# Two attention chunks run as halves of 64 tokens, with a new order of all operations

## The chip, the core and the metric

The kernel runs on one core of one Trainium2 chip. The metric is the time of one execution on the device, in microseconds (us). A core has engines with instruction streams of their own, each worked off in order: TensorE (PE; its weight loads are PEld), VectorE (DVE), ScalarE (ACT), GpSimd (POOL), and SyncE (SP), which here issues the transfers (DMA).

## The reference

Three layers, one after the other, on q, k, v of 2 batches, 8 heads, 768 tokens and 64 columns in float32:

```
# 1. attention with decay, blocks of 64 tokens, per head
intra = (q_b @ k_b.T * Dmask) @ v_b ;  inter = (q_b * lam_pow) @ kv_state
out   = intra + inter
kv_state = lam**64 * kv_state + (k_b * rev_pow).T @ v_b
# 2. channel mix: x_prev is x shifted by one token, d_ff = 1024
xk, xr = mu_k*x + (1-mu_k)*x_prev, mu_r*x + (1-mu_r)*x_prev
x = sigmoid(xr @ w_r) * (relu(xk @ w_k)**2 @ w_v)
# 3. gated convolution with 5 taps
y = (sigmoid(conv(x)) * (x @ w_val)) @ w_out
```

The weights of layers 2 and 3 arrive as 64-bit floats.

## The kernel before

**Chunks.** Attention runs over 12 chunks of 128 tokens, 0 to 5 for the first batch and 6 to 11 for the second, each for all 8 heads. A chunk has operations named by a letter and its number: Tk and Tq (PE transposes of k and q, chunks 0 to 5 only), Ek and Eq (ACT copies of these out of PSUM), Q (q times powers of lam), D (k times decays), S (scores), M (DVE: scores times the mask), U (the update of the state), O and N (state times decay, plus the update), Z (the result; for halves Y and Z), X (the result copied to SBUF). The function `whole` treats the chunk as one block of 128 tokens; `halves` treats it as two blocks of 64. `BIG` says which chunks are whole:

```
676         x, keep_x = (whole if c < BIG else halves)(c, b, cc)
494                     e.matmul(su[:, s, C * n:C * n + C], kt[half[s], n, :], qt[half[s], n, :], ...)
571                         e.matmul(su[half[j], s, Q * n:Q * n + Q], kt[half[s], n, t], qt[half[s], n, t], ...)
```

In `whole`, S is 8 products of 128 by 128 tokens (L494), U 8 (L516), Z 16 (L553), M one DVE multiplication of 128x1024 (L501), and the state is multiplied and added once (O at L531, N at L534). In `halves`, S is 16 products of 64 by 64 tokens (L571), U 16 (L592), Y 8 and Z 24 (L655), M 128x512 (L578), and there are two pairs of O and N, named O2.0, N2.0, O2.1, N2.1 (L613, L616). Z of halves begins with a drain of PE (L662). Each float32 product is two instructions in the trace. Both write their scores to the PSUM tile su and their result to xx. The update of `halves` lies in su too, that of `whole` in a buffer of its own.

**Weights.** A piece of 128x512 64-bit numbers is loaded (w0 to w19; y and z for layer 3) and turned into a high and a low float32r part by steps a to f, h and l: a, b and h on ACT, c, d and e on DVE, f and l on DVE or POOL. w0 to w3 belong to w_r, w4 to w11 to w_k, w12 to w19 to w_v.

**Products.** The channel mix goes over three groups of 512 tokens (pr 0, 1, 2). mr and mk are the mixed inputs (steps a, b, h, l); r, k and v the products, where `k0.2.1` is group 0, block 2, second half of the sum. A unit is 6 matmuls of 128x512 (12 of 128x256 for r of group 0), a third each for high by high, high by low, low by high. g are the gates (DVE), a and p the products of layer 3. Their accumulators turn in 4 PSUM buffers.

**Order.** ORDER is a list, written out in the source, of all 1070 operations; each engine gets its own in that sequence, with the engine after the colon where there is a choice (V, A, G for DVE, ACT, POOL). A load waits in SP's stream until its SBUF buffer is free. An operation on POOL waits for the last DVE operation that stands before it in the list (L249 to L254).

Of the kernel before, what the change touches and what calls it, by code (L numbers as in the profile page):

```python
# [18 lines left out]


ORDER = """
    zero table eye lam scan warm7 w3 w3b w3a w3c w3d w3e w1 w2 w1a w2a q0 Tq0 w1b warm3 w3f:V
# [11 lines left out]
    mr0.2.1h mr0.2.1l:V w9 w6d mk0.2a:A mk0.2b v5 mk0.0h w7c w7b Z4 w6b mk0.0l:V k6 r0.10.0
    r0.10.1 r0.10s mk0.1h mk0.2h w7d mk0.3b r0.11.0 w5l:V w6e mk0.1l:V w7e r0.11.1 mk0.3h
    mk0.3l:V w9a w7f:V r0.11s w9c w6f:V r0.00s w8 w7h mk0.2l:V w8a w8c w11 w6h w7l:V w11a
    w6l:V D6:V w10a w10c O5.0:V U5 v6 w9d w8d k0.2.0 w10b w13 k0.0.0 w9e X4:A w11c w13b w11b
# [2 lines left out]
    k0.1.1 w9l:V w12a w11f:V k0.2e:A k0.0q:A jq3.0 jk3.2 w12c w10f:V w11h w12d w11l:G jk3.3  # L40
    X5:A Bq3 w10h jk3.1 w10l:V w13d k0.0l:V jk3.0 k0.1e:A k0.1h w12e k0.6.0 N6.0:A k0.2h
    O6.1:V H2:A k7 w12f:V w13e k0.1q:A k0.2q:A k0.4.0 Q6:G Bk3 k0.5.0 k0.5.1 k0.5e:A k0.7.0
    k0.5h w13f:V k0.7.1 k0.1l:V S6 k0.7e:A w12h D7:G H3 k0.7h N6.1 w15 M6 w15a w14 w13h w15b
    v7 k0.5q:A w14a w12l:V k0.3h k0.3q:A Q7:V w15c Y6 k0.4.1 w13l:V w15d k0.6.1 Z6 O7.0:V w14c
    S7 w15e w14b w14d w15f:V w14e U7 k0.3l:V w17 k0.4e:A X6:A w14f:G w16 k0.6e:A M7 w15h w18
    v0.3.0 w19 N7.0 w17a v0.0.0 w15l:V k0.6h w17c w16a w16c w14h w17d v0.1.0 Y7 w16d k0.4h
    k0.4q:A Z7 v0.2.0 X7:A w18a w14l:V jk4.0 v9 k0.2l:V w16e w17e k0.4l:V w16b w19b w16f:V x0
    w18c k0.5l:V v0.2.1 k0.7q:A w17b w17f:V w16h v0.3.1 w19a w19c w16l:V w17h jq4.3 w18b
    w17l:V H4:A w18d v0.1.1 w19d mk1.1a:A w18e w19e w18f:V mk1.3a:A v0.0.1 w19f:V k0.6q:A
    mk1.0a:A k0.6l:V v0.2.2 k0.7l:V jk4.2 w18h w19h w19l:V w18l:V jk4.1 jq4.1 v0.0.2 v0.1.2  # L50
    mk1.0b v0.3.2 mk1.2a:A mk1.3b v0.1.3 mr1.1a:A v0.0.3 v0.2.3 mk1.0h mk1.1b k8 mk1.0l:V
# [6 lines left out]
    k1.4.1 k1.5.1 mr1.1l:G k1.2e:V mr1.2a:A O10.0:V k1.2h N10.0 O10.1:G N10.1 Q10:V M10 k1.6.1
    X9:V k11 D11:V k1.1q:V z3 mr1.2b mr1.2h mr1.2l:G r1.3.0 k1.0q:V x1.3:A v11 Y10 S11 k1.4e:A
    k1.4h Z10 X10:A U11 x1.2:A k1.7h mr1.3h O11.0:V N11.0 M11 k1.6e:A k1.1l:V mr1.3l:G k1.6h  # L60
    r1.1.0 k1.2q:V z0 k1.5e:A Y11 Z11 X11:V H5:G r1.2.0 mk2.0a:V x3 mk2.0b r1.2.1 mk2.0h
    r1.3.1 k1.0l:V mk2.1a:V mk2.1b k1.3h k1.3q:A k1.4q:G r1.2s r1.1.1 r1.1s v1.3.0 r1.3s y0
    r1.0.0 r1.0.1 mk2.3a:A v1.0.0 k1.2l:G k1.3l:V v1.3.1 k1.4l:G mk2.2a:V k1.5h y0a mk2.2b
    k1.5q:V z3a k1.5l:V v1.2.0 r1.0s k1.7q:A v1.0.1 k1.6q:V k1.6l:G k1.7l:V v1.1.0 v1.1.1
    v1.1.2 z0a z0c mr2.1a:A z0d mk2.1h mk2.0l:G mr2.0a:V mr2.3a:V y3 y3a y3c mr2.1b y3d mk2.2h
    y0c v1.2.1 mk2.1l:G mk2.3b v1.1.3 v1.1e v1.0.2 v1.0.3 v1.0e mr2.1h mr2.1l:V mk2.3h mr2.3b
    mk2.3l:V y2 y2b v1.2.2 v1.3.2 v1.2.3 y2a k2.1.0 mk2.2l:G y2c cw cwb cwa k2.4.0 cwc v1.2e
    cwd x4.2:V v1.3.3 k2.4.1 cwe cwf:V mr2.0b z3c x1.1:A z3d y1b v1.3e k2.2.0 z3e k2.4e:A y0d
    cwg cwt y1a y1c y1d y1e y3b z3b k2.1.1 g1.2.0:A z3f:V y0e mr2.2a:V k2.6.0 y2d y2e k2.1e:V
    g0.2.0:A mr2.0h k2.3.0 k2.3.1 k2.6.1 x2.3:V y1f:V z0e k2.5.0 g1.3.0:A g1.3.1 g0.3.0:A y0b  # L70
    k2.3e:A y0f:G g1.3.2 k2.5.1 y2f:G k2.5e:V k2.7.0 mr2.3h k2.6e:A k2.0.0 mr2.2b k2.3h k2.0.1
    x1.0:V k2.3q:A mr2.0l:G mr2.2h mr2.2l:V k2.2.1 k2.0e:A k2.3l:V k2.4h x2.1:A y3e y3f:V
    r2.3.0 k2.2e:A g0.2.1 mr2.3l:V g0.3.1 k2.7.1 k2.2h k2.0h g0.1.0:A g0.3.2 g0.3.3 x2.0:V
    g0.1.1 g0.1.2 k2.0q:A k2.2q:A k2.2l:V r2.1.0 k2.1h z0b k2.0l:V r2.2.0 r2.2.1 r2.1.1 r2.2s
    r2.0.0 r2.0.1 g1.0.0:V k2.1q:V k2.1l:V r2.3.1 k2.7e:A k2.7h g1.0.1 k2.5h k2.5q:V k2.5l:V
    g1.0.2 r2.0s k2.7q:A k2.4q:A z0f:V r2.3s s0.0h k2.6h v2.0.0 y1h v2.2.0 g1.2.1 g1.2.2
    v2.1.0 k2.4l:V v2.1.1 g1.3.3 g1.3.4 y2h r2.1s v2.3.0 y1l:V g0.2.2 v2.0.1 k2.7l:V v2.3.1
    g0.1.3 g0.0.0:A v2.3.2 v2.1.2 y2l:V v2.0.2 v2.2.1 v2.2.2 z1 k2.6q:V k2.6l:V v2.3.3
    g1.1.0:A y3h g1.1.1 z1a z1c g1.3s g0.0.1 y0h s0.2h s1.1h y0l:V g0.0.2 y3l:V s1.3h s1.1l:V
    z2 g1.0.3 s1.0h s0.0l:G g1.0.4 g0.0.3 g0.1.4 g0.1s s1.0l:G v2.1.3 s1.2h v2.1e v2.3e s0.1h  # L80
    z3h v2.0.3 s1.3l:V s0.3h s0.1l:V s1.2l:V g0.0.4 v2.2.3 g0.0s s0.2l:V a1.3.0 z0h g1.2.3
    a1.0.0 v2.0e a1.3.1 s0.3l:G a1.3e z1d z1e g1.0s a1.0.1 a1.0e z2a z3l:G a0.0.0 g0.2.3 z2c
    g0.2.4 a0.2.0 g0.2s z2d a0.1.0 a0.1.1 a0.1e z2e a0.2.1 z0l:V g1.2.4 z1b z1f:V z2b a0.3.0
    a0.0.1 a0.2e a0.3.1 a0.0e a0.2h a0.0h g0.3.4 a0.2l:V g0.3s z2f:G x5.1:A a1.2.0 a1.1.0
    v2.2e a0.1h a1.1.1 a0.3e a0.1l:V a0.3h x5.0:A a1.2.1 z2h a0.3l:V a0.0l:V z1h z1l:V z2l:V
    p0.0.0 x4.0:A p0.0.1 g1.1.2 g1.1.3 x5.2:A g1.1.4 g1.2s a1.3h p0.0e:V a1.3l:G g1.1s
    g2.2.0:A x4.3:A a1.1e a1.0h s2.2h g2.0.0:V p0.1.0 p0.1.1 p1.1.0 p1.0.0 g2.0.1 p0.1e:A
    g2.0.2 a1.1h a1.1l:V p1.0.1 p1.1.1 a1.0l:V x4.1:A g2.1.0:A a1.2e a1.2h g2.1.1 p2.1.0
    x5.3:V g2.3.0:A p0.0o p1.1e:A a1.2l:V s2.1h p1.0e:A g2.0.3 g2.3.1 g2.3.2 p2.1.1 g2.3.3
    g2.3.4 g2.3s p2.1e:A s2.1l:V p0.1o p3.1.0 s2.0h p3.1.1 g2.0.4 g2.0s p3.0.0 p3.0.1 p1.1o  # L90
    p3.1e:A p3.1o g2.1.2 s2.0l:V a2.1.0 g2.1.3 p2.0.0 p2.0.1 g2.1.4 a2.0.0 p3.0e:A g2.2.1
    g2.2.2 g2.2.3 a2.2.0 s2.3h s2.2l:G s2.3l:V a2.1.1 g2.2.4 p3.0o a2.0.1 g2.2s g2.1s a2.1e
    a2.0e a2.2.1 a2.1h a2.2e a2.3.0 a2.1l:V a2.3.1 a2.0h a2.0l:V a2.3e p4.0.0 a2.2h a2.2l:V
# [1000 lines left out]
```

## Time and profile before

| | |
|---|---|
| median of 3 runs | 290.45 us (290.04 to 290.76) |
| profiled execution | 290.39 us, of which 288.6 us from the first to the last instruction (the span) |
| PE busy | 275.2 us (95%) |
| DVE, ACT, POOL busy | 235.4 us (82%), 164.1 us (57%), 49.3 us (17%) |
| granted TensorE clock | 1.000 in every slice |
| chain that ended last | 90% PE, 5% DMA, 3% DVE |

The profile is one execution. A time in it counts from the span's first instruction; 1.8 us of the execution's own time lie around the span. The chain is followed back from the last instruction, at each step to what released it or to the instruction before it on its engine.

### The profile page before, as it was taken

The numbers are of one execution on the slowest core, as the hardware profiler recorded it, in microseconds if no ns is written. First come the engines' busy times: TensorE is split into PE (matmuls) and PEld (weight loads), VectorE is DVE, ScalarE is ACT, GpSimd is POOL, SyncE is SP. The second block draws the span as 40 slices with busy tenths as digits, with TensorE's granted clock in tenths as the row PEclk, the third lists the DMA queues.
The fourth block names the chain that finished last, engine by engine and source line by source line (L and its number), as shares of the span: only waits on it lengthen the run. The fifth ranks groups of instructions, "written<-read, shape, count | busy, mean of one in ns | idle before, by whom it ended". The sixth has DMA issues, their size and how long they took to land.

```text
span 288.6 us, 5971 instructions
## 1 busy us (share of the span) xinstructions
PE 275.2 (95%) x2345; PEld 229.1 (79%) x2345; DVE 235.4 (82%) x402; ACT 164.1 (57%) x309; POOL 49.3 (17%) x59
## 2 busy tenths in 40 slices
...
DMA packets 63626, 29.25 MB, mean 101 GB/s; under 512 B 58322, under 2 KB 58606, under 8 KB 63598
## 3 DMA queue, kind: packets, MB, share of 16 engines
...
q14 instruction: 10, 0.08, 0.1%
HBM read 25.72 MB, written 3.15 MB: 100 GB/s over the span
## 4 chain that ended last, share of the span: by engine, by line
PE 90%; DMA 5%; DVE 3%; ACT 1%; issue 1%; SPq 0%; DVEq 0%; ACTq 0%
PE b_k L754 23%; PE b_v L754 23%; PE b_r L754 12%; PE b_p L942 11%; PE b_a L754 11%; PE xx L655 4%; DMA b_v<-in_v_dram 2%; DMA xx<-in_moe_w_r_dram 2%; PE su L592 2%; PE su L571 1%; PE su L494 1%; PE xx L553 1%; PE b_Tq L440 1%; DVE xx L342 0%; DVE b_k L480 0%
## 5 line engine op out<-in xcount | busy, mean ns | idle before, releaser
L894 DVE SCALAR_TENSOR_TENSOR b_g<-xx,cw,b_g 128x512 f32<-128x512 f32 x48 | 38.5, 810 | 0.6
L754 PE MATMUL b_k<-b_mk_2h,w_rk 128*128 128x512 f32 x48 | 19.0, 397 | 0.0
L754 PE MATMUL b_r<-b_mr_0h,w_rk 128*128 128x256 f32 (+1 forms) x80 | 19.0, 312 | 0.0
L754 PE MATMUL b_k<-b_mk_0h,w_rk 128*128 128x512 f32 x48 | 18.9, 394 | 0.0
L754 PE MATMUL b_k<-b_mk_3h,w_rk 128*128 128x512 f32 x48 | 18.7, 390 | 0.0
L754 PE MATMUL b_k<-b_mk_1h,w_rk 128*128 128x512 f32 x48 | 18.7, 390 | 0.0
L902 ACT ACTIVATE b_g<-b_g 128x512 f32<-128x512 f32 x12 | 7.4, 628 | 16.6 <-DVE b_g L894 16.5
L754 PEld LDWEIGHTS b_r<-b_mr_0h,w_rk 128*128 128x128 f32 x80 | 13.2, 191 | 0.9
L869 DVE TENSOR_TENSOR xx<-b_v,xx 128x512 f32<-128x512 f32 x12 | 8.0, 687 | 6.4 <-PE b_v L754 6.4
L754 PE MATMUL b_r<-b_mr_0l,w_rk 128*128 128x256 f32 (+1 forms) x40 | 12.2, 305 | 0.0
L616 DVE TENSOR_TENSOR state<-su,state 128x256 f32<-128x256 f32 x13 | 5.5, 424 | 6.4 <-PE su L571 3.6
L754 PEld LDWEIGHTS b_k<-b_mk_2h,w_rk 128*128 128x128 f32 x48 | 9.0, 188 | 2.0
L754 PEld LDWEIGHTS b_k<-b_mk_0h,w_rk 128*128 128x128 f32 x48 | 9.0, 188 | 1.9
L754 PEld LDWEIGHTS b_k<-b_mk_3h,w_rk 128*128 128x128 f32 x48 | 9.0, 188 | 1.9
L754 PEld LDWEIGHTS b_k<-b_mk_1h,w_rk 128*128 128x128 f32 x48 | 9.0, 188 | 1.9
L440 PE MATMUL b_Tq<-ident,b_q 128*128 128x128 f32 x24 | 4.3, 309 | 5.6 <-DMA b_q<-in_q_dram 5.6
L754 PE MATMUL b_v<-b_k_0h,w_v 128*128 128x512 f32 x24 | 9.6, 399 | 0.0
L330 ACT ACTIVATE xx<-xx 128x512 int32<-128x512 uint32 x12 | 7.9, 668 | 2.9 <-DMA xx<-in_moe_w_r_dram 2.9
L754 PE MATMUL b_v<-b_k_1h,w_v 128*128 128x512 f32 x24 | 9.4, 391 | 0.0
L754 PE MATMUL b_k<-b_mk_2l,w_rk 128*128 128x512 f32 x24 | 9.4, 390 | 0.0
L754 PE MATMUL b_k<-b_mk_3l,w_rk 128*128 128x512 f32 x24 | 9.4, 390 | 0.0
L754 PE MATMUL b_k<-b_mk_0l,w_rk 128*128 128x512 f32 x24 | 9.4, 390 | 0.0
...
## 6 DMA issues: line engine op xcount, KB each, us to landing
...
```

The costliest lines, as they stand in the source:

```text
L330: op(f"{key}b", "A", lambda e: e.activation(words(I32, 0), words(U32, 0), AF.Copy, scale=2.0 ** -29), reads=[raw], writes=[low])
L440: e.transpose(ps()[:, C * n:C * n + C], src()[:, C * n:C * n + C], ident)
L494: e.matmul(su[:, s, C * n:C * n + C], kt[half[s], n, :], qt[half[s], n, :], start=True, stop=True,)
L553: e.matmul(x[half[b_], a, s, :], w, m, start=a == 0 and kind == (0 if cc else 1), stop=kind == a == 1,)
L592: e.matmul(su[half[s], j, c0:c0 + D], kt[half[j], 2 * n + s if c < PE_CHUNKS else h, :], vt[half[j], h, :], start=True, stop=True,)
L616: op(f"N{c}.{j}", "V", lambda e, u=u, t=state_of[new]: e.tensor_tensor(t, u, t, op=ALU.add), reads=[su_b[f"u{j}"]], writes=[st_b[new]])
L655: last = e.matmul(x[half[b_], j, at, :], w, m, start=spots[i] not in spots[:i], stop=spots[i] not in spots[i + 1:],)
L754: e.matmul(o, r(a), r(b), start=first and n == 0, stop=last and n == len(todo) - 1)
L869: op(f"v{pr}.{rb}e", "V", lambda e: e.tensor_tensor(x2_at(pr, rb), two(ps), x2_at(pr, rb), op=ALU.mult), reads=[ps], writes=[x2_b[pr, rb]])
L894: e.scalar_tensor_tensor(t, src, w, t, op0=ALU.mult, op1=ALU.add)
L902: op(f"g{pr}.{n}s", "A", lambda e: e.activation(acc(), acc(), AF.Sigmoid), writes=[acc])
L942: e.matmul(at(ps), x, w, start=u == 0 and n == 0, stop=u == 1 and n == 5)
```

## The change

`BIG` becomes 2: chunks 2 and 3 go through `halves`. That removes O2, N2, O3, N3 and adds Y2, Y3 and O, N for each half; Q2, D2, Q3 and D3 use the decays of 64 tokens. The list is another one from its first to its last line: 1075 operations, two warm-up operations on PE (warm0, warm7) in place of three (warm7, warm3, warm2), other places for all else, and other engines for some: 62 operations on POOL instead of 46, 378 on DVE instead of 392. The first loads are lam, w0, w7, w2, w1, mu, q0, k0, where they were lam, w3, w1, w2, q0, k0. No function is new; shown are the parts of the list before the first products, at the last weights of w_v, and around chunk 8.

```
--- before.py
+++ after.py
 ORDER = """
-    zero table eye lam scan warm7 w3 w3b w3a w3c w3d w3e w1 w2 w1a w2a q0 Tq0 w1b warm3 w3f:V
-    w3h k0 w1c w1d w2c Tk0 k1 w1e w2d w0 Eq0:A w1f:V kd0 w2b Tk1 w2e w3l:V w2f:V Ek0:A D0:V
-    warm2 w0a w0b v0 S0 q1 U0 w1h D1:V w2h k2 N0:A Tq1 w0c q3 pows:G Ek1:A Eq1:A w0d w0e w0f:G
-    Tk2 M0 w1l:V S1 Q1 w2l:V Ek2:A D2:G M1 q2 quar Z0 Tq2 O1:V w0h Eq2:A w0l:V Q2 Tq3 Eq3:A Q3
-    v1 k3 X0:A U1 N1 S2 Tk3 kd1 Z1 Ek3:A D3:G w4 M2 O2:V w4a X1:A S3 mu w4b muT H0 H1:G w4c
-    w4d w4e w4f:G v2 muc mr0.1.0a:A mr0.3.0a:A U2 M3 N2 k4 Tk4 w4h mr0.1.0b mr0.0.0a:A O3:V
-    mr0.2.0a:A q4 Z2 X2:A Tq4 mr0.1.0h w4l:V mr0.0.0b v3 mr0.3.0b w5 mr0.2.0b U3 N3 Eq4:A D4:V
-    O4.0:V Ek4:A mr0.0.0h mr0.1.0l:V v4 mr0.0.0l:V mr0.3.0h mr0.3.0l:V Z3 Q4 w5a S4 X3:A w5c
-    U4 N4.0 O4.1:G r0.00.0 M4 mk0.3a:A mr0.3.1a:A mr0.3.1b k5 Tk5 q5 mr0.1.1a:A Tq5 w5d
-    r0.01.0 mr0.1.1b w5b mr0.0.1a:A mr0.2.0h mr0.0.1b w5e Eq5:A mr0.2.0l:V mk0.0a:A Ek5:A
-    mr0.2.1a:A cw0 mk0.0b D5:G mk0.1a:A Y4 mr0.0.1h w7 w7a S5 r0.01.1 N4.1 mr0.1.1h M5
-    mr0.2.1b mr0.3.1h mk0.1b w5f:V r0.00.1 mr0.1.1l:V mr0.0.1l:V w6 w6a mr0.3.1l:V w5h w6c w10
...
-    k0.3.0 k0.3.1 N5.0 k0.3e:A jq3.1 w13a w8e w13c k0.0.1 w9b w8b Q5 r0.01s k0.0e:A w10d w9f:V
...
-    mk1.3l:V k1.0.0 mk1.2l:V N7.1 O8.0:G v10 k1.3.1 k1.1.0 jq4.2 k1.0.1 jk4.3 jq4.0 jq5.1 v8
-    D8:G U8 Bq4 Q8:V D9:V Bk4 S8 N8.0 O8.1:G M8 Y8 N8.1 Z8 O9.0:G mr1.0a:A k1.0e:A k1.0h S9
...
+    zero eye lam table scan w0 w0a w7 w0c H0 w7a w7c w2 pows:G w1 w0b w0d w2a w7b w7d quar w1a
+    w0e w7e w1b mu muT w2c w7f:V w2d warm0 w0f:V warm7 w2b q0 Tq0 w1c w0h k0 q2 q1 Tk0 w7h w2e
+    kd0 Eq0:A w1d w2f:V w1e Ek0:A Tq2 Eq2:A S0 w7l:V k2 kd1 w0l:V w2h w1f:V Tq1 k1 Tk1 Eq1:A
+    Q2 v0 w3 D0:G Tk2 U0 v1 M0 Ek1:A Q1 D1:V w1h D2:V w1l:V S1 N0:A w3a Z0 w3b U1 w2l:G M1 w5
+    muc w3c w3d X0:A v2 Ek2:A O1:V w5a w3e Z1 X1:A N1 w3f:V w5c S2 O2.0:V w3h w5d mr0.3.0a:A
+    mr0.2.0a:A mr0.1.0a:A U2 N2.0 Y2 q3 O2.1:G k3 M2 mr0.3.0b N2.1 Tq3 mr0.1.0b Eq3:A k4 Tk3
+    Q3 Ek3:A Z2 mr0.3.0h mr0.1.0h mr0.2.0b mr0.0.0a:A D3:V Tk4 mr0.1.0l:V S3 O3.0:V mr0.0.0b
+    D4:G X2:A v3 U3 q4 Tq4 N3.0 M3 Y3 mr0.0.0h O3.1:V mr0.0.0l:V Eq4:A Ek4:A Z3 H3 N3.1 v4
+    H1:G Q4 U4 w5e O4.0:V q5 w3l:V S4 Tq5 k5 X3:A mr0.1.1a:A Tk5 r0.00.0 r0.01.0 mk0.1a:A
+    mr0.3.0l:G mr0.2.0h M4 Ek5:A N4.0 mr0.0.1a:A mr0.2.0l:V mk0.1b mr0.1.1b w4 w4a mk0.0a:A
+    mr0.0.1b r0.00.1 w4c mk0.0b v5 mr0.2.1a:A w4d mr0.2.1b mr0.3.1a:A mr0.3.1b mr0.1.1h
+    mr0.1.1l:V Eq5:A O4.1:V mk0.1h mk0.1l:V w6 mr0.0.1h mr0.0.1l:V w5b w4e D5:G Y4 Z4 w8 S5 M5
+    jq3.0 w6a N4.1 mk0.2a:A w4b mr0.2.1h w6c mk0.3a:A w4f:V w5f:V mr0.3.1h r0.01.1 mr0.2.1l:V
...
+    mk1.2a:A w19f:V k0.6l:V v0.0.1 v0.3.2 v0.0.2 w18h w18l:V v0.2.2 v0.1.2 w19h w19l:V jq4.2
...
+    mk1.0l:V v0.2.3 x3 mk1.1l:G O7.1:G v0.0e mk1.3h k10 v0.3.3 D8:G v0.2e k1.5.0 jk4.3 v0.3e
+    N7.1 k1.1.0 O8.0:G v0.1e mk1.2b k1.2.0 Bq4 k1.4.0 jk4.0 U8 mr1.1a:A mk1.3l:G mk1.2h Bk4 S8
+    mr1.2a:A mk1.2l:V k1.5.1 k1.2.1 k1.2e:A N8.0 Q8:G Y8 M8 Z8 D10:V x1.0:A mr1.3a:A O8.1:V k9
...
 """
...
-    BIG = 4
+    BIG = 2
```

## Rows read from the trace of the kernel before

**Rows 1.** The page's part 1: busy us, share of the span, instructions.
```profile
PE 275.2 (95%) x2345; PEld 229.1 (79%) x2345; DVE 235.4 (82%) x402; ACT 164.1 (57%) x309; POOL 49.3 (17%) x59
```

**Rows 2.** The chain that ended last: start us, us, what.
```profile
20.86 0.61 PE b_U L516 x16
21.48 1.09 PE su L494 x16
...
23.16 1.62 PE xx L553 x32
...
32.81 0.70 PE su L592 x32
33.51 1.62 PE b_r L754 x12
35.13 0.44 PE b_Tk L440 x4
...
37.43 0.39 PE xx L655 x16
37.82 0.66 PE su L571 x32
...
49.27 9.74 PE b_k L754 x42
...
82.12 17.91 PE b_v L754 x78
...
107.45 0.51 PE su L571 x32
...
108.53 0.46 PE xx L655 x16
108.99 0.11 issue
109.10 0.93 PE xx L655 x48
...
123.51 0.47 PE su L592 x32
```

**Rows 3.** DVE in order of time: start us, us, operation.
```profile
16.29 1.22 DVE L501 TENSOR_TENSOR b_M<-su,b_scan 128x1024 f32<-128x1024 f32 x1
17.42 0.93 DVE L348 TENSOR_TENSOR w_rk<-xx,w_rk 128x512 fp32r<-128x512 f32 x1
...
24.80 0.43 DVE L333 TENSOR_SCALAR b_w4a<-b_w4a 128x512 f32<-128x512 f32 x1 [0.17 <-ACT b_w4a L328]
25.26 0.43 DVE L336 TENSOR_SCALAR b_w4a<-b_w4a 128x512 int32<-128x512 int32 x1
...
33.62 0.42 DVE L616 TENSOR_TENSOR state<-su,state 128x256 f32<-128x256 f32 x1
33.95 0.68 DVE L578 TENSOR_TENSOR b_M<-su,dmaskq 128x512 f32<-128x512 f32 x1
34.55 0.48 DVE L734 SCALAR_TENSOR_TENSOR b_mr_0a<-b_X,rest,b_mr_0a 128x256 f32<-128x256 f32 x1
...
92.87 1.30 DVE L348 TENSOR_TENSOR w_v<-b_w,w_v 128x512 fp32r<-128x512 f32 x2
```

**Rows 4.** Transposes at 10 to 12 and 22 to 24 us: ns min/median/max, first and last start.
```profile
L440 PE MATMUL b_Tk<-ident,b_k x7: 421/421/422, 10.6 to 11.9; 128*128 128x128 f32 x7
L440 PE MATMUL b_Tk<-ident,b_k x4: 273/273/332, 22.5 to 22.9; 128*128 128x128 f32 x4
```

**Rows 5.** Groups by line on POOL: busy us, mean ns, idle before.
```profile
L881 POOL TENSOR_TENSOR b_s_0l<-xx,b_s_0h 128x512 fp32r<-128x512 f32 x2 | 3.4, 1718 | 28.6 <-PE b_v L754 28.6
```

**Rows 6.** PE's weight loads in order of time, the second half of k2.
```profile
16.61 0.20 PEld L440 LDWEIGHTS b_Tk<-ident,b_k 128*128 128x128 f32 x2 [0.34 <-DMA b_k<-in_k_dram]
```

**Rows 7.** Two stretches: length, busy PE, PEld, DVE, ACT, POOL, granted clock, DMA share, GB/s.
```profile
10.00:11.00 1.00, 1.00 (x6) 1.00 (x6) 1.00 (x3) 1.00 (x4) 0.00 (x0) 1.00 1.12 246
...
14.00:16.00 2.00, 1.92 (x34) 1.49 (x30) 1.93 (x5) 2.00 (x5) 0.00 (x0) 1.00 1.32 217
```

More of the change, by code (lines that the diff above doesn't have):

```diff
@@ L34 @@
[L34 to L37, printed above, removed]
-    k0.3.0 k0.3.1 N5.0 k0.3e:A jq3.1 w13a w8e w13c k0.0.1 w9b w8b Q5 r0.01s k0.0e:A w10d w9f:V
-    k0.1.0 k0.2.1 Y5 w8f:V w8h jq3.3 Z5 w9h w11d w10e w11e w12 w12b U6 k0.0h w8l:V jq3.2
@@ L40 @@
[L40 to L51, printed above, removed]
@@ L52 @@
-    mk1.2b mk1.1h mk1.1l:V mk1.3h v0.2e v0.3.3 x2.2:A O7.1:G mk1.2h v0.1e k9 v0.0e k1.3.0
-    mk1.3l:V k1.0.0 mk1.2l:V N7.1 O8.0:G v10 k1.3.1 k1.1.0 jq4.2 k1.0.1 jk4.3 jq4.0 jq5.1 v8
-    D8:G U8 Bq4 Q8:V D9:V Bk4 S8 N8.0 O8.1:G M8 Y8 N8.1 Z8 O9.0:G mr1.0a:A k1.0e:A k1.0h S9
-    k1.3e:A jk5.2 U9 N9.0 jq5.3 jq5.0 jq5.2 k1.7.0 k1.1.1 mr1.0b mr1.0h k1.1e:A k1.7.1 M9
-    jk5.0 mr1.1b k1.2.0 k10 k1.2.1 mr1.3a:A Bq5 Q11:V k1.7e:A v0.3e k1.4.0 mr1.3b O9.1:V N9.1
-    jk5.3 D10:V mr1.1h jk5.1 k1.1h k1.6.0 X8:V mr1.0l:V y1 k1.5.0 Q9:V Y9 Z9 U10 Bk5 S10
@@ L58 @@
[L58 to L93, printed above, removed]
@@ L94 @@
-    p5.2.0 p4.1.0 p1.0o a2.3h a2.3l:V p4.0.1 p4.0e:A p2.0e:V p2.0o p2.1o p4.1.1 p4.1e:V p5.2.1
-    p5.0.0 p4.1o p4.0o p5.0.1 p5.2e:V p5.2o p5.0e:A p5.1.0 p5.1.1 p5.1e:A p5.0o p5.1o
+    zero eye lam table scan w0 w0a w7 w0c H0 w7a w7c w2 pows:G w1 w0b w0d w2a w7b w7d quar w1a
+    w0e w7e w1b mu muT w2c w7f:V w2d warm0 w0f:V warm7 w2b q0 Tq0 w1c w0h k0 q2 q1 Tk0 w7h w2e
+    kd0 Eq0:A w1d w2f:V w1e Ek0:A Tq2 Eq2:A S0 w7l:V k2 kd1 w0l:V w2h w1f:V Tq1 k1 Tk1 Eq1:A
+    Q2 v0 w3 D0:G Tk2 U0 v1 M0 Ek1:A Q1 D1:V w1h D2:V w1l:V S1 N0:A w3a Z0 w3b U1 w2l:G M1 w5
@@ new lines @@
+    mr0.0.1b r0.00.1 w4c mk0.0b v5 mr0.2.1a:A w4d mr0.2.1b mr0.3.1a:A mr0.3.1b mr0.1.1h
+    mr0.1.1l:V Eq5:A O4.1:V mk0.1h mk0.1l:V w6 mr0.0.1h mr0.0.1l:V w5b w4e D5:G Y4 Z4 w8 S5 M5
+    jq3.0 w6a N4.1 mk0.2a:A w4b mr0.2.1h w6c mk0.3a:A w4f:V w5f:V mr0.3.1h r0.01.1 mr0.2.1l:V
+    mr0.3.1l:V mk0.0h w6d mk0.0l:V w4h w6e w6b w5h w5l:V w9 mk0.3b w4l:V r0.01s w9a w6f:V
+    jk3.3 r0.11.0 U5 mk0.2b w9c w8b r0.10.0 w10 w8a w9b mk0.3h r0.00s w8c r0.11.1 r0.10.1
+    r0.10s O5.0:V w9d w6h w8d jk3.0 mk0.3l:V w11 w6l:V r0.11s k0.2.0 jk3.1 mk0.2h w9e mk0.2l:V
@@ new lines @@
+    jk3.2 w9f:V w8e w10b w10a k0.0.0 k0.1.0 w11a w11c w10c w8f:G w9h k0.3.0 jq3.1 w13 w11b Bk3
+    k0.2.1 w10d w8h w9l:V k0.2e:A k0.2h k0.0.1 w10e w8l:V w13a k0.3.1 k0.1.1 k0.1e:A k0.1h
+    jq3.3 w10f:V X4:A jq3.2 w12 w13c k0.5.0 w11d H2:A Q5 w11e w11f:G N5.0 k0.4.0 k0.0e:A Bq3
+    k0.7.0 w13d w10h k0.3e:A w10l:V w13b k6 v6 w13e k0.1q:A Q6:V w12a k0.2q:A k7 w12c D6:V
+    w11h k0.6.0 w12b Y5 k0.0h S6 w11l:V k0.2l:V w12d Z5 X5:A w13f:V U6 k0.0q:A w12e k0.4.1 w14
+    N6.0:A O6.1:V k0.6.1 w13h k0.6e:A k0.0l:V w12f:G Y6 w15 w12h k0.7.1 k0.3h M6 w15a N6.1
@@ new lines @@
+    w13l:V Q7:V D7:V k0.1l:V k0.7e:A k0.5.1 w15c w14a w12l:V w15d w14c w15e k0.7h Z6 S7 v7
+    w14d w14b O7.0:V U7 v0.1.0 w15b w15f:V v0.2.0 k0.3q:A w14e k0.3l:V w14f:G k0.5e:A X6:A
+    w15h M7 k0.4e:A w17 w17a w16 N7.0 w16a w17c w16c w15l:V w18 w16d w14h w14l:V w17d w16e
+    v0.3.0 k0.4h k0.4q:A w17e v0.0.0 jk4.1 Y7 jq4.1 Z7 w17b k0.4l:V w19 w16b w18a w16f:V
+    w17f:V k0.5h k0.5q:A k0.5l:V w16h v0.3.1 v0.1.1 w18c w17h w19b w18b w16l:V w17l:V v9 w19a
+    w18d w19c k0.7q:A w18e w19d jq4.3 w18f:V w19e k0.7l:V X7:A mk1.0a:A k0.6h v0.2.1 k0.6q:A
@@ new lines @@
+    mk1.2a:A w19f:V k0.6l:V v0.0.1 v0.3.2 v0.0.2 w18h w18l:V v0.2.2 v0.1.2 w19h w19l:V jq4.2
+    mk1.3a:V v8 jk4.2 mk1.3b v0.1.3 mk1.1a:A mk1.1b mk1.1h jq4.0 mk1.0b v0.0.3 k8 mk1.0h
+    mk1.0l:V v0.2.3 x3 mk1.1l:G O7.1:G v0.0e mk1.3h k10 v0.3.3 D8:G v0.2e k1.5.0 jk4.3 v0.3e
+    N7.1 k1.1.0 O8.0:G v0.1e mk1.2b k1.2.0 Bq4 k1.4.0 jk4.0 U8 mr1.1a:A mk1.3l:G mk1.2h Bk4 S8
+    mr1.2a:A mk1.2l:V k1.5.1 k1.2.1 k1.2e:A N8.0 Q8:G Y8 M8 Z8 D10:V x1.0:A mr1.3a:A O8.1:V k9
+    D9:G N8.1 U9 mr1.3b k1.5e:A jk5.3 S9 jk5.1 k1.1.1 k1.7.0 k1.7.1 k1.7e:A mr1.0a:V k1.1e:A
@@ new lines @@
+    jq5.3 jq5.1 mr1.2b mr1.2h O9.0:V M9 y0 k1.0.0 N9.0 mr1.1b Q9:G v10 mr1.1h k1.4.1 H4:G
+    k1.6.0 O9.1:V cw0 k1.3.0 jk5.2 jk5.0 X8:A Y9 Bk5 jq5.2 Z9 jq5.0 Bq5 Q10:V N9.1 S10 O10.0:V
+    U10 cw v11 N10.0 k1.3.1 z1 z1b k11 k1.6.1 k1.0.1 M10 X9:A mr1.0b Y10 x1.1:V O10.1:V N10.1
+    D11:G U11 mr1.0h Z10 mr1.1l:V mr1.3h k1.6e:A k1.6h mr1.0l:V z1a H5:A O11.0:V S11 mr1.3l:G
+    y3 y3b r1.0.0 k1.4e:A k1.3e:V k1.0e:V k1.3h k1.3q:G X10:A r1.2.0 r1.1.0 mr1.2l:V z2 k1.2h
+    M11 k1.0h k1.6q:A cwa cwc cwd cwe k1.1h k1.1q:A r1.3.0 Q11:G k1.7h r1.2.1 r1.1.1 N11.0 Y11
```

34 lines of the change are left out of this document (added).

## The prediction

> **What bounds the kernel now.** The page's first part comes first: PE is busy 275.2 of 288.6 us, DVE 235.4 [rows 1]. The chain of waits says where that matters: from 33.51 us on it is almost one run of PE work, to the end [rows 2]. One stop is in it: chunk 8's scores end at 107.96 (107.45 and 0.51) and its Y starts at 108.53, 0.57 us later, since the state's first half is not yet there; a drain of 0.11 in each halves chunk is the rest [rows 2]. So after 33.5 us the time is the sum of PE's work, and before it, it is a question of when the first product can start.
>
> There the timeline of DVE is the one to read. From 3.7 to 94.2 us DVE has hardly a gap, and the reader is to see how its starts follow each other: an operation of 128x256, or a one-input one of 128x512, takes 0.33 us from start to start (33.62 to 33.95), a two-input one of 128x512 0.60 (33.95 to 34.55), the mask of a whole chunk 1.13 (16.29 to 17.42), and one that needs the result of the one right before it 0.12 more (24.80 to 25.26 is 0.46) [rows 3]. At 94.17 the last low part of w_v (w18l) ends [rows 3]; the four units of v that need it are 24 of the 78 matmuls which end at 100.03, at 17.91/78 = 0.23 us each, so they start at 94.5 [rows 2]. DVE was done 0.35 us before PE asked. Up to there DVE and PE are both tight; a change that helps one alone gives little.
>
> **The chunks.** A whole chunk costs PE 1.09 (S), 0.61 (U) and 1.62 (Z), together 3.32 us; a halves chunk 0.47 (S, taken from the U of the same number and size), 0.47 (U), 0.39 (Y), 0.11 (drain) and 0.93 (Z), together 2.37 [rows 2]. For two chunks PE loses 2 x 0.95 = 1.9 us of work. On DVE the two masks get shorter by 2 x (1.13 - 0.60) = 1.06, and each chunk has a second O and N, 0.33 each, one of these four on POOL [rows 3]. So the chunks alone change DVE by 1.0 - 1.06, nothing.
>
> **The start.** The new list does more of DVE's work in another order, so I count it. The first product (r0.00.0) stands behind U4, S4, Tq5 and Tk5 on PE, and U4 behind N3.1, which reads the same PSUM tile. Up to N3.1 DVE has 51 operations in the new list; up to N4.0 in the old one also 51. By kind the new one has one more of 0.33, one more of 0.60, two fewer of 1.13, and seven fewer pairs in which one waits for the one right before it (1 instead of 8): 0.33 + 0.60 - 2.26 - 0.84 = -2.2 us. N4.0 ended at 33.62 + 0.42 = 34.04 [rows 3], so N3.1 ends at 31.9, if DVE is slowed and kept waiting as much as before. Then U4 0.70, S4 0.66 and the two transposes, 0.44 each [rows 2], 2.2 us: r0.00.0 starts at 34.1. Before it started at 33.5, but Tq5 and Tk5 came after it.
>
> The loads allow that, if barely. Ahead of r0.00.0 stand the same six weights and 17 attention loads as ahead of Tk5 before, and Tk5 ran at 35.13 with nothing to wait for [rows 2]. Its load lands between the 34.1 above (no cost) and 35.1 (1.0 us); I take no cost, since two 128 KB halves need about 1.2 us at the 217 GB/s of a stretch of attention loads [rows 7], and by the old list's last loads SP stood waiting for buffers.
>
> From r0.00.0 to the first unit of k it took 49.27 - 33.51 = 15.76 us [rows 2], of which Tk5 and Tq5, 0.88, are now ahead. Y4, Z4 and S5 now stand together; a group of attention work between products costs about 0.2 more than one among its like (0.66 against 0.47 [rows 2]), so 0.2 less: 14.7. The first unit of k starts at 48.8, 0.5 us earlier than before.
>
> **The middle.** From there to 100.03 the products are the same ones and the attention groups as many, so PE keeps its 0.5, if DVE keeps up. Up to w19l, now the last, DVE has 168 operations where it had 164 up to w18l: three more of 0.33, three more of 0.60, two fewer of 1.13 and the seven pairs, -0.3: 93.9. PE asks at 94.5 - 0.5 = 94.0. So the 0.5 just stands, and the rest of the 1.9 us can't come out, for DVE would be late.
>
> **Chunk 8.** The new list has k1.5.1 and k1.2.1 between S8 and Y8; two units are 12 x 0.23 = 2.8 us, so N8.0 has time and the 0.57 goes. It makes one group more, 0.2. Gain 0.4.
>
> **The rest.** After chunk 8 PE has the same units in another order. 16 more operations run on POOL there, at up to 1.72 us for one of 128x512 [rows 5] against 0.60 on DVE. I cost this at nothing: following the new list, each of their results stands at least three units (4.1 us) ahead of its reader, with two exceptions, s0.1l before a0.0.0 and a2.2l before p5.2.1, which have 4.1 and 4.8 us for chains of 3.3. If a cover fails it is 1 us at each place (bounds 0 and 2). No gain is to be had, since PE had no gaps there. The tail, p5.1 and its transfer, is unchanged.
>
> **Sum.** 0.5 + 0.4 = 0.9 off the profiled execution's 290.39, which lies 0.06 under the median of 290.45: 289.5 us, 0.3% faster. A difference of 0.3%, 0.87 us here, is about what a measurement of this kernel can tell from none.
>
> **The rivals.**
>
> PE's whole saving comes out. The 1.9 us show if DVE's idle and slowed time shrinks too: its instructions up to w18l sum to 86.7 us by the start-to-start times above, and it took 94.17 - 3.71 = 90.5, so 3.8 are waits and slowing (0.93 for a low part while POOL works [rows 3]). For it speaks that seven dependent pairs are gone; against it, that each new N and O waits for PE or POOL in turn. 290.4 - 1.9 - 0.4 = 288.1.
>
> DVE is late. If the new waits cost DVE 1 us more, w19l comes at 94.9, the units of v start 0.9 late, and only chunk 8's gain stays: 290.4 + 0.4 - 0.4 = 290.4. No change.
>
> TensorE is slow at the start (the other side). Transposes took 421 ns each at 10 to 12 us and 273 at 22 [rows 4], although the granted clock reads 1.00 there [rows 7]; in between PE had worked without a long gap, with warm3 and warm2 between the transposes. In the new list both warm-ups stand ahead of Tq0 and behind muT, which waits for a transfer, and each transpose waits for its load. The same 3.67 MB that ended with k2 at 16.61 before [rows 6] now end with k1; then comes v0, at about 17.8, and behind it U0, S1, Z0, U1, Z1, S2 and U2, some 5 us of work at the fast rate, until N2.0, which DVE reaches at about 25. At the slow rate this work grows by a half (421/273) to twice, 2.5 to 5 us, and the slack is 1.5 to 2: N2.0 and all behind it 1 to 3.5 us late. 290.5 to 293, say 291.8. It decides itself at Tk1 and Tk2, near 17 us: if these take 421 still, it happens. Against it: a load lands every 1.2 us, so PE is not idle for long.
>
> The Trainium skill ("TensorE: Matmul & The Clock Gate", Part 1) has this as a rule: the slow state is the default and sustained matmul activity releases it. By that rule the start of this list, with its fillers gone, is a risk; the trace agrees in that the transposes got faster only after a stretch of work.
>
> A cover after 100 us fails, as above, at one place: 289.5 + 1.5 = 291.0. "SBUF — State Buffer" of the Trainium skill ("Who interferes with whom") says that of DVE and GpSimd the later one on their shared port pair blocks fully; by that, more work on POOL would hold up DVE for up to an operation each. The trace shows less: the low part that began at 17.42 took 0.93 instead of 0.69.
>
> **How the numbers follow.** The forecast, 0.45, with 288.8 to 290.3 of its own: a little over half of it lies under 289.6. PE's whole saving 0.17. DVE late 0.13. Slow TensorE 0.15, two thirds of it over 291.3. A failed cover 0.10, a third of it over 291.3; the middle of the loads' bounds adds to both sides. Faster by over 0.3%: 0.26 + 0.17 + 0.01 = 0.44. Slower: 0.10 + 0.04, and 0.08 for loads or buffers late by more than their bound: 0.22. Within: 0.34. The range of 8 in 10 reaches from the second case to the middle of the slow one: 287.9 to 291.9.
>
> **What would show it.** In the new profile: DVE without gaps to 94; N3.1 ending near 31.9 and r0.00.0 starting near 34.1; the first unit of k at 48.8; no wait ahead of Y8; PE without a gap after that; 273 ns for the transposes of chunk 1. Wrong it would be if Tk5 waits for its load beyond 35, if PE waits for DVE's low parts between 48 and 94, or if a wait for POOL stands in the chain after 100.

## The result, and the profile after

The changed kernel takes 294.16 us (median of 5 runs, 293.62 to 295.83) against 290.45 us, a ratio of 1.014 (95% interval 1.0103 to 1.0177). It is slower by 3.7 us where 289.5 was forecast, and lies outside the range. The profiled execution is one of the longer ones, 295.38 us with a span of 293.6. Some executions of a kernel fall in a slower state (below, three of twelve with the chunks alone and one of six with 64 instructions); the medians given hold them, the ratios leave them out.

PE is busy as long as before, with more instructions ([rows 1]):

```profile
PE 274.0 (93%) x2469; PEld 228.9 (78%) x2469; DVE 229.1 (78%) x388; ACT 165.3 (56%) x311; POOL 73.5 (25%) x75
```

The chain that ended last shows where the time goes (start us, us, what; compare [rows 2]):

```profile
30.50 0.45 PE su L592 x27
30.95 2.21 issue
33.16 0.48 PE su L592 x5
33.64 1.04 PE b_Tq L440 x4
34.68 0.64 PE xx L655 x16
...
35.43 1.56 PE xx L655 x48
36.99 0.85 PE su L592 x32
37.84 0.63 PE su L571 x21
38.47 0.29 issue
38.76 0.69 PE su L571 x11
39.45 0.70 PE b_Tq L440 x4
40.15 0.44 PE b_Tk L440 x4
40.59 4.31 PE b_r L754 x36
...
54.97 16.36 PE b_k L754 x72
```

Three things are to be seen. PE stops in the middle of an operation: after 27 of the 32 matmuls of U3 (two for each product) it does nothing for 2.21 us, and "issue" says that it waited for nothing the profile shows; the same again for 0.29 us within S4. Second, what follows runs slowly: Y and Z of chunk 3 take 0.64 and 1.56, where [rows 2] have 0.39 and 0.93. Third, r0.00.0 starts at 40.59, not at 34.1, and the first unit of k at 54.97, 5.7 us later than before. From there to the end of the span the changed kernel needs 238.6 us and the one before 239.3: all of the loss is ahead of 55 us.

The granted clock explains the second (stretches of 2 us; length, busy PE, PEld, DVE, ACT, POOL, granted clock, DMA share, GB/s; [rows 7] are the same view):

```profile
30.00:32.00 2.00, 0.95 (x59) 0.82 (x55) 1.25 (x4) 0.85 (x2) 0.62 (x1) 1.00 1.31 231
32.00:34.00 2.00, 0.84 (x7) 0.72 (x7) 0.31 (x1) 0.00 (x0) 0.42 (x1) 0.71 0.71 178
34.00:36.00 2.00, 1.89 (x40) 1.38 (x42) 2.00 (x6) 1.09 (x2) 0.26 (x2) 0.50 0.48 152
36.00:38.00 2.00, 2.00 (x88) 2.00 (x83) 1.85 (x4) 0.91 (x2) 0.38 (x2) 0.50 0.03 8
38.00:40.00 2.00, 1.71 (x33) 1.41 (x26) 0.52 (x1) 1.12 (x3) 0.71 (x1) 0.58 0.94 256
```

TensorE falls to its lower level, 1.2 GHz (0.50), within the long stop and is back at 2.4 GHz just ahead of 40 us; 0.71 and 0.58 are the stretches in which it changed. The five executions nearly order themselves by this: a mean granted clock of 0.988, 0.988, 0.994, 0.993 and 1.000 with 295.83, 295.38, 294.16, 293.81 and 293.62 us. The one at full clock still loses 3.2 us. The 2.2 us between it and the longest go with the clock, but may be longer stops in part: only one of the five has a trace.

DVE's waits up to 45 us (waiting operation, what it waited for, us in total, times, longest) show both ends of the matter:

```profile
DVE state L616 <- PE su L592: 2.4, 1, 2.4
DVE b_M L578 <- PE su L571: 1.6, 1, 1.6
DVE b_w7a L333 <- ACT b_w7a L328: 1.2, 1, 1.2
```

N3.0 waits for U3, M4 for S4: DVE now waits for PE's stops. The third wait is at the start, and new as well: the second weight's first step has nothing to work on until 7.85 us.

**What stops PE.** Counting helps more than naming. All matmuls and weight loads of PE up to the first stop, and from there to the second:

```profile
0.00:30.95 30.95, 17.82 (x344) 15.62 (x345) 25.86 (x53) 21.36 (x44) 7.22 (x20) 1.00 1.03 236
30.95:38.50 7.55, 5.20 (x127) 4.38 (x126) 4.45 (x10) 2.92 (x6) 2.18 (x4) 0.62 0.53 127
```

344 + 345 = 689, and 127 + 126 = 253 more. (With PE's waits and drains counted too, the trace has 705 and 961 instructions up to the two stops, 256 apart; the expectations below use these numbers.) And the queue of "instruction" transfers, which is otherwise no part of the story, brings a packet of 0.02 MB at 30.4 us (queue, packets, MB, share; from 30.4 to 30.5 us):

```profile
q8 instruction: 1, 0.02, 78.6%
```

Theory A: PE's own instructions come in blocks, and PE stands at the end of one until the next is there. A halves chunk is made of twice as many instructions as a whole one, for less time: 64 + 64 + 32 + 96 matmuls and weight loads in 2.37 us, against 32 + 32 + 64 in 3.32, counted from [rows 2] with a weight load for each matmul. The Trainium skill ("Runtime: NRT & Kernel Launch", Instruction fetch mechanics) says that an engine's instructions are refilled in blocks of 16 KiB, which are 256 instructions, and that this is mostly hidden. The block size fits (253 that the view counts, and waits and the like beside them); "hidden" does not, here. Theory B, the rival: the new list, with its order of loads and DVE work, loses the time, and what looks like a stop is a wait of another kind.

### The profile page after: what moved, and what is told of

Read it like the earlier page. It is cut to its first block, busy times and chain, and to the rows that moved or that the text cites. A ratio compares the mean times of both kernels' runs of the same rounds, so it can differ in the third digit from the quotient of the medians.

```text
span 293.6 us, 6235 instructions
## 1 busy us (share of the span) xinstructions
PE 274.0 (93%) x2469; PEld 228.9 (78%) x2469; DVE 229.1 (78%) x388; ACT 165.3 (56%) x311; POOL 73.5 (25%) x75
## 4 chain that ended last, share of the span: by engine, by line
PE 89%; DVE 4%; DMA 3%; issue 2%; SPq 0%; ACT 0%; DVEq 0%
PE b_k L754 23%; PE b_v L754 22%; PE b_r L754 12%; PE b_p L942 11%; PE b_a L754 11%; PE xx L655 5%; DMA xx<-in_moe_w_r_dram 2%; PE su L592 2%; PE su L571 2%; DMA b_q<-in_q_dram 1%; DVE xx L342 1%; PE b_Tq L440 1%; DVE w_rk L348 1%; PE b_Tk L440 0%; DVE b_M L501 0%
## 5 line engine op out<-in xcount | busy, mean ns | idle before, releaser
L894 DVE SCALAR_TENSOR_TENSOR b_g<-xx,cw,b_g 128x512 f32<-128x512 f32 x48 | 40.0, 852 | 3.5 <-ACT b_g L896 2.9
L480 POOL TENSOR_TENSOR b_k<-b_k,kdec 128x512 f32<-128x512 f32 x6 | 6.5, 1081 | 31.2 <-DVE state L616 10.3
L655 PEld LDWEIGHTS xx<-b_Q,state 64*64 64x64 f32 x304 | 7.0, 142 | 7.4 <-issue 5.3
L655 PE MATMUL xx<-b_Q,state 64*64 64x64 f32 x304 | 9.8, 241 | 2.6 <-DVE state L616 1.5
L616 DVE TENSOR_TENSOR state<-su,state 128x256 f32<-128x256 f32 x17 | 7.1, 416 | 4.7 <-PE su L592 3.5
L592 PE MATMUL su<-b_v,b_k 64*64 64x64 f32 x288 | 7.6, 232 | 2.2 <-issue 2.2
L613 DVE TENSOR_TENSOR state<-state,pw 128x256 f32<-128x256 f32 x14 | 5.8, 417 | 4.7 <-PE xx L655 4.7
```

The costliest lines, as they stand in the source:

```text
L480: return e.tensor_tensor(t, t, kdec[:, int(c >= BIG), int(c < PE_CHUNKS)].unsqueeze(2).to_broadcast([P, H, D]), op=ALU.mult,)
L592: e.matmul(su[half[s], j, c0:c0 + D], kt[half[j], 2 * n + s if c < PE_CHUNKS else h, :], vt[half[j], h, :], start=True, stop=True,)
L613: op(f"O{c}.{j}", "GV", lambda e, a=state_of[new], o=state_of[old]: e.tensor_tensor(a, o, pw[:, :, Q - 1:Q].to_broadcast([P, NPAIR, D]), o ...
L616: op(f"N{c}.{j}", "V", lambda e, u=u, t=state_of[new]: e.tensor_tensor(t, u, t, op=ALU.add), reads=[su_b[f"u{j}"]], writes=[st_b[new]])
L655: last = e.matmul(x[half[b_], j, at, :], w, m, start=spots[i] not in spots[:i], stop=spots[i] not in spots[i + 1:],)
L894: e.scalar_tensor_tensor(t, src, w, t, op0=ALU.mult, op1=ALU.add)
```

## The experiments

Each ran beside the kernel before on the same chip; a ratio is to that one. Two kernels load less, as said there; the others compute the whole reference.

**The chunks alone.**

```
-    BIG = 4
+    BIG = 2
```

in the list of before, with Y2, Y3 and the O and N of each half (all on DVE) put where O, N and Z of these chunks stood, kd1 ahead of D2, and D2 and O4.0 a little later.

> Chunks 2 and 3 as halves, in the list of before with the fewest changes. Theory A (PE's instructions come in blocks of 256 from memory, each some 5.6 us after the block before was begun while loads run, and halves need 256 instructions where a whole chunk needs 128): one or two stops of PE that the trace puts down to issue, between 29 and 40 us, at instruction 705 and 961 of PE; r0.00.0 starts at 35.5 to 37.5 instead of 33.5, and the time is 292 to 294 us. Theory B (the new list's order of DVE work and loads is the loss): no such stops, r0.00.0 near 33.5, 290 to 291 us.

292.14 us, ratio 1.0052 (1.0030 to 1.0074). No stop by "issue": the waits of PE are

```profile
PE xx L655 <- DVE state L616: 2.6, 2, 1.4
```

Y2 and Y3 wait for N2.0 and N3.0, since N on DVE now stands between a chunk's U and its Y, and after that the clock is 0.72 and 0.50 at 32 to 36 us. The time was in A's range, but not for A's reason; the changed kernel's wait of 1.5 us ahead of Y2 (26.7 us) is of this kind.

**The list alone.**

```
-    BIG = 2
+    BIG = 4
```

in the new list, with O2, N2, O3, N3 in the places of O2.0, N2.0, O3.0, N3.0, and the rest of the halves left out.

> The new list with chunks 2 and 3 whole, so with 256 fewer instructions on PE ahead of the first product. Theory A: no stop of 2 us inside U3, at most one under 1 us further on; the clock stays at 1.0; r0.00.0 at 35 to 36.5 and 290.5 to 292 us, what is left being DVE's later start. Theory B: still 293 to 294.5 us.

291.14 us, ratio 1.0020 (1.0002 to 1.0039); r0.00.0 at 36.06, clock 1.0. B alone would have kept the loss. One stop by "issue" is left, 0.20 us at 41.95 us. Up to 41.8 us, just ahead of it, there are

```profile
0.00:41.80 41.80, 28.58 (x470) 25.18 (x471) 36.76 (x75) 30.71 (x64) 8.99 (x23) 1.00 1.01 244
```

470 + 471 = 941 = 689 + 252 matmuls and weight loads: the stop is in S5, where no other kernel stops, but at a block's end.

**128 more instructions.**

```
+    def pad(e):
+        for _ in range(32):
+            e.matmul(pad_ps()[0:8, 0:8], ident[0:8, 0:8], ident[0:8, 0:8], start=True, stop=True)
+    op("pad", "P", pad, reads=[ident_b], writes=[pad_ps])
...
-    zero eye lam table scan ...
+    zero eye pad lam table scan ...
```

> The changed kernel with 32 products of 8x8 (128 PE instructions) more, in PE's idle time before 10 us. Theory A: the stops follow the count of instructions and not the work: they come 128 instructions earlier in the work, before or in S3 instead of inside U3, and in U4 instead of S4; since each block still takes as long, the time stays within 1 us of 294.2. Any theory that ties the stop to an operation, a buffer or a transfer: the stop stays inside U3.

291.02 us, ratio 1.0018 (0.9995 to 1.0041): more work on PE, and 3 us faster than the changed kernel. The stops didn't move, they went; that the time would stay was wrong. The chain in the head, where 29.1 and 32.9 us are the places of the block ends:

```profile
33.46 0.69 PE su L592 x32
34.16 0.47 PE su L571 x32
34.62 0.59 PE b_Tq L440 x4
35.21 0.44 PE b_Tk L440 x4
35.65 4.30 PE b_r L754 x36
...
50.03 16.39 PE b_k L754 x72
```

The blocks' transfers began at 24.5 and 29.8 us here, each less than 1 us after PE had passed the end of the block before, and in the changed kernel at 30.4 and 36.3, over 3 us after.

**256 more instructions** (64 in place of 32 above), which puts the blocks back where they were.

> The changed kernel with 64 small products (256 PE instructions, twice as many as in the padded run before) in PE's idle time before 10 us. Theory A (instructions come in blocks of 256): the blocks lie at the same places of the work as in the changed kernel again, so the stop comes back inside U3, at PE instruction 961 in place of 705, with 2 us or more, and the time goes back to 293.5 to 294.7 us. Rival (the small products help by themselves, by keeping PE awake or by a later start of the rest): 291 us or less, as with 128, and no stop.

295.35 us, ratio 1.0165 (1.0134 to 1.0196). The stop is back, after 27 matmuls of U3, 2.15 us long, and a second in S4 (the chain, then the counts):

```profile
30.40 0.45 PE su L592 x27
30.85 2.15 issue
33.00 0.33 PE su L592 x5
...
37.55 0.68 issue
```

```profile
0.00:30.90 30.90, 20.93 (x472) 18.25 (x472) 25.91 (x53) 21.48 (x44) 7.73 (x20) 1.00 0.94 235
30.90:37.60 6.70, 4.42 (x126) 3.82 (x126) 4.39 (x10) 2.94 (x6) 1.67 (x3) 0.76 0.59 148
```

944 = 689 + 255, then 252. Between 128 and 256 instructions of the same small work lie 4.3 us. Whatever else padding does (keeping PE awake, delaying the rest), 256 do more of it than 128, and yet the gain is gone: so it is the count.

**DVE's start.**

```
-    zero eye lam table scan w0 w0a w7 w0c H0 w7a w7c w2 pows:G w1 w0b w0d w2a w7b w7d quar w1a
-    w0e w7e w1b ...
+    zero eye lam table scan w0 w0a w7 w0c H0 w0b w0d w0e w7a w7c w2 pows:G w1 w2a w7b w7d quar w1a
+    w7e w1b ...
```

> The changed kernel with w0's steps b, d and e ahead of w7's a and c, so that DVE does not wait 1.24 us for the second weight. If DVE paces the head to 26 us: w7c ends its wait with DVE 0.8 to 1.2 us further on, Y2's wait for N2.0 (1.51 us) shrinks by as much. Theory A: PE's stop in U3 takes over part of it, and the time falls by 0 to 1.0 us, to 293.2 to 294.2. If DVE alone is the loss: 293.0 or less.

294.45 us, ratio 1.0130 (1.0094 to 1.0165), no gain. DVE reached N2.0 0.54 us sooner, and PE stopped after the same 689 instructions, 2.21 us, and 252 later for 0.96 where it was 0.29. Within PE's limit a faster DVE buys a longer stop.

**Both: 128 instructions and DVE's start**, the powers of lam moved as well (`lam table pows:G scan`).

> The padded kernel with 128 instructions, and DVE's start mended: w0's steps b, d, e ahead of w7's, and the powers of lam on POOL as soon as lam is there, during the scan, instead of beside DVE's first weight steps. If DVE sets the end of the head once PE has its instructions: N2.0 starts 1.0 to 1.7 us sooner than 26.2, r0.00.0 at 34.2 to 35.0 instead of 35.65, and 289.5 to 290.3 us against 291.0. If something else (loads, ACT) sets it: within 0.3 us of 291.0.

291.05 us, ratio 1.0015 (0.9997 to 1.0033). DVE was ready for N2.0 at 25.3 us, 0.9 sooner, and waited 0.87 us for PE, which had stopped for 0.95 us within S2 at 24.1, 218 + 219 = 437 = 689 - 252 instructions into its stream. The clock read 0.50 behind it, from 27.4 to 30.8 us, a stop of 0.23 us followed after 941, and r0.00.0 came at 36.97, not at the 34.2 to 35.0 that were expected. The head is not set by DVE alone any more: the stop has moved to the block before.

**64 and 192 instructions with DVE's start, and 192 without.**

> The kernel with DVE's start mended, padded with 64 PE instructions instead of 128, so that the blocks begin 64 instructions later in the work: in chunk 2's Y or Z and chunk 4's U. Theory A: where PE stops depends on this count alone, and the time differs from the 291.05 us of 128 by what its stops change: without any stop 289.6 to 290.3 us, with one of 2 us 292 to 293. Rival (the head's end is set by loads or DVE and the count matters no more): 291.0 within 0.3.

295.20 us, ratio 1.0137 (1.0098 to 1.0176), three stops in the head, 0.83, 1.35 and 2.34 us:

```profile
0.00:24.50 24.50, 13.78 (x218) 12.12 (x219) 20.64 (x40) 17.11 (x35) 6.31 (x19) 1.00 1.06 246
24.50:30.30 5.80, 4.18 (x126) 3.40 (x126) 5.13 (x13) 4.29 (x10) 0.62 (x1) 1.00 0.91 198
30.30:35.20 4.90, 3.36 (x126) 2.71 (x125) 3.43 (x9) 2.14 (x5) 1.66 (x3) 1.00 0.76 189
```

437, then 252, then 251: U2, S3 and U4, three different operations, one count. The time fits neither answer: it was to be 292 to 293 us with a stop of 2 us, and there were three stops.

> The same with 192 instructions of padding: blocks begin 64 instructions sooner in the work than with 128, in Z0 to U1 and in chunk 2's Z. Theory A: as for 64, 289.6 to 290.3 us without a stop, 292 to 293 with one of 2 us. Rival: 291.0 within 0.3.

293.09 us, ratio 1.0095 (1.0063 to 1.0126); in the profiled execution, the shortest of six at 291.67, stops of 0.52 us after 941 instructions and of 0.93 one block later.

> The changed kernel with 192 instructions of padding and nothing else. Theory A: the stop is not inside U3; whole head without a stop 290.8 to 291.3 us as with 128, with one at another place 292 to 294.5. Rival (anything but the count): as with 128, 291.0, or as with 256, 295.

292.71 us, ratio 1.0093 (1.0063 to 1.0124), one stop of 0.54 after 941, again in the shortest execution. That a stop sits at a block's end held in every run; how long it is, theory A did not foretell.

**The same padding in the kernel before** (the 128 instructions after `eye`).

> The kernel before with the same 128 small instructions in PE's first idle time. In its head 256 instructions take 5.7 us at the least and mostly 7, so theory A has no stop to take away: the time of before within 0.3 us. Rival (the padding helps any kernel, by waking PE or by delaying something): 0.5 us or more faster.

291.15 us, ratio 1.0029 (1.0011 to 1.0047). No gain, so padding as such gives nothing; but 0.8 us of loss, which was not expected. There is no stop by "issue" in its head; in the profiled execution, the longest, PE waits 2.2 us for k, where it waited 0.2 before.

**Lighter loads**, to see why the block is late. Of q4, v4, q5 and k5 (then v3 too) 32 of 128 tokens are loaded and the rest is set to zero by POOL, so what depends on them is not computed:

```
...
+        m = 32 if f"{nm}{c}" in LIGHT else C
-        rows = slice(cc * C, cc * C + C)
+        rows = slice(cc * C, cc * C + m)
...
+            if m < C:
+                nc.gpsimd.memset(t()[32:64], 0.0)
+                nc.gpsimd.memset(t()[64:128], 0.0)
...
```

> The changed kernel, of q4, v4, q5 and k5 only 32 of 128 tokens loaded, the rest set to zero by POOL (so its results for these chunks are not the reference's): 480 KB less to load from 26 to 30 us, the order of instructions unchanged. Theory A with the fetch queued behind the loads: the fetch of the block that begins at instruction 705 starts before 29 us instead of at 30.45, the stop inside U3 shrinks from 2.2 us to under 1, and the time falls to 291 to 292.5 us. Rival (the fetch takes this long by itself): the stop stays at 2 us, 293.5 us or more.

295.20 us, ratio 1.0169 (1.0138 to 1.0200). The four tiles are 256 KB each, so 768 KB fell away, not 480. The transfer of the block began at 29.4, 1 us sooner, and the stop in U3 was 1.3 us; then Tq4 waited 1.0 us for POOL's zeros, which spoils the time, and the stop in S4 was 1.2 us. The time that was expected, 291 to 292.5, did not come.

> The changed kernel, of v3, q4, v4, q5 and k5 only 32 of 128 tokens loaded and the rest set to zero by POOL ahead of D4, so that POOL does not hold up PE as in the lighter run before (its results for these chunks are not the reference's). All that is loaded from 25 to 29 us is a quarter. If the fetch waits behind the loads: the block of instruction 705 starts to come within 1 us of PE passing instruction 449 (3.56 us in the changed kernel), PE's stop at 705 is gone or under 0.3 us, and the time is 290.5 to 292 us. If the fetch takes its 3 us whatever else is loaded: the stop at 705 stays at 2 us and the time at 293.5 us or more.

293.49 us, ratio 1.0085 (1.0054 to 1.0117); v3 and q4 stand ahead of D4 here. Neither answer: the block came at 29.3, the stop was 1.02 us, less than half, and the clock stayed at 1.000. And the block after it was late too, with a stop of 0.97 us: PE passed the block's end at 31.96, the transfer began at 34.3, and for most of the time between nothing was loading:

```profile
32.50:34.30 1.80, 1.67 (x68) 1.30 (x66) 1.80 (x6) 1.09 (x2) 0.16 (x3) 1.00 0.00 0
```

the DMA share is 0.00. So loads are a part of the delay, and not all of it.

**The changed kernel again**, on the chip of the run above.

> The changed kernel once more, on the chip and in the hour of the lighter one. Theory A: stops put down to issue at PE instructions 705 and 961 again and nowhere else, 2 us or more together, and 293.5 to 295.5 us.

295.67 us, ratio 1.0168 (1.0125 to 1.0212): stops of 2.48 and 0.56 us, after 689 instructions and 252 later, the clock at 0.53 from 34 to 36 us.

**Chunk 8 alone**, in the list of before.

```
-    D8:G U8 Bq4 Q8:V D9:V Bk4 S8 N8.0 ...
+    D8:G U8 Bq4 Q8:V D9:V Bk4 S8 k1.1.1 N8.0 ...
...
-    ... k1.7.0 k1.1.1 mr1.0b ...
+    ... k1.7.0 mr1.0b ...
```

> The kernel before with k1.1.1 moved between chunk 8's scores and its Y, nothing else. By the prediction's step: the stop of 0.57 us ahead of Y8 is gone and a group more costs 0.2, so 0.4 us less than before, 290.0 to 290.3. Rival (the stop only moves to the next N or Y): no difference.

289.93 us against 290.61, ratio 0.9977 (0.9960 to 0.9994): the one version that beats both kernels. The wait is gone, and PE goes through:

```profile
107.48 0.47 PE su L571 x32
107.94 1.59 PE b_k L754 x6
109.54 0.39 PE xx L655 x16
```

## Why the prediction was wrong

**The step that failed is the one on the start.** It put N3.1's end at 31.9 and r0.00.0, 2.2 us behind it, at 34.1. In the changed kernel N3.1 ended at 35.70 and r0.00.0 came 4.9 us later, at 40.59: 6.5 us late, in three terms.

- *PE's instructions, a term that the sum did not have.* The parts on chunks counted PE's time, 1.9 us less, and not the instructions that it takes. The stop of 2.21 us is DVE's 2.4 us wait ahead of N3.0. Shown by the count: the stops stand after 437, 689, 941 or 1193 matmuls and weight loads (within some 3) in every kernel that has them, whatever operation lies there, and go with 128 more instructions and come back with 256. The kernel before passes the same count at 33.1 us, in the middle of U4 and right ahead of r0.00.0, whose 12 matmuls take 1.62 us [rows 2]; the changed one has some 265 more to do ahead of r0.00.0, and passes it in U3. How much PE can get is seen where it has run dry: from the end of one stop to the end of the next, one block later, it is 5.60 us in the changed kernel (33.16 to 38.76), and 5.1 to 6.8 us in the eight traces that have two such stops. A halves chunk uses 256 instructions in 2.37 us; two whole chunks, with as many, take 6.64.
- *The clock that follows.* From 34 to 38 us it is 0.50. Z3 takes 0.63 more than a Z at full rate and ends at 36.99, so that U4 starts 1.3 us after N3.1's end and not at once; U4, S4 (with its stop) and Tq5 take 0.15, 0.95 and 0.26 more than was taken for them. That is the 2.7 us between 2.2 and 4.9. The rival of a slow TensorE, with 1 to 3.5 us of lateness, holds these 2.7, but had the wrong place and the wrong reason: it was to be decided at Tk1 and Tk2, and there the transposes took the fast rate of [rows 4]:

```profile
L440 PE MATMUL b_Tk<-ident,b_k x8: 272/273/273, 17.1 to 17.9; 128*128 128x128 f32 x8
```

  The cost came not from idling between loads at the start but after a stop of two us in the densest part. (At the start both kernels are slow: transposes still take 421 ns at 14.6 us in the changed one. The 1.00 that [rows 7] read at 10 us is no measurement of the clock: the trace's record of it begins at 13.9 us, at 15.8 in the changed kernel.) The Trainium skill ("TensorE: Matmul & The Clock Gate", Part 1) has sustained activity as what releases the throttled clock; the trace agrees, with 0.50 from within the stop to 39.7 us and 1.00 after that stretch of work.
- *DVE's start*, 1.2 us. "If DVE is slowed and kept waiting as much as before" did not hold: w7's first step waits 1.24 us for its load and ACT, where DVE before had no such wait. With the stops gone, by 128 more instructions, N3.1 ended at 33.36, 1.5 us after 31.9, and r0.00.0 came at 35.65, 1.5 after 34.1; that DVE's start makes up most of this is read from the wait and not shown. With 192 instructions the mended start had N3.1 done 0.7 us sooner than without, in one trace each, and no version gained time by it.

**What held.** From r0.00.0 to the first unit of k it took 14.4 us (14.7 forecast). PE has no wait from there to the end, the low parts of w_v included; no POOL cover failed. Chunk 8 gave 0.7 us by itself and some 0.7 in the changed kernel behind 55 us (238.6 against 239.3), 0.4 having been forecast: the interval of the run, 0.2 to 1.2 us, holds that. PE's smaller work bought nothing, as forecast.

**What each half of the change is worth.** The list alone costs 0.2% (0.02 to 0.39), the chunks alone 0.5%, both with the stops taken away 0.2% (-0.05 to 0.41), both as they are 1.4 to 1.7%. Most of the loss is in neither half but in what they make together: 256 instructions more, in a stretch where they follow each other without products between. That the chunks alone, with as many instructions, pass without a stop is a sign that the place of a block's end and the time of its transfer count, and not the number alone.

**What stays open.** Why a block is late: its transfer began 0.1 us (with 128 instructions more) to 3.9 us (in the repeat) behind PE's passing of the block before, and 6.9 us in the trace with 128 instructions and DVE's start, where PE passed 185 matmuls and weight loads at 15.66 us and the transfer came at 22.5. Loads at a quarter took 1 us off one of them, and another waited 2.4 us with hardly a load running. After a stop's end the next transfer never began sooner than 1.8 us. Nor was it tried to make the head of the changed kernel need fewer instructions, other than by taking the halves back, which theory A would ask for. Why the padding cost the kernel before 0.8 us was not settled; a shift of its loads is what the one profile shows.
